# Two 512-column GpSimd reductions in place of one of 1024, and the instruction order planned anew, in a fused linear-attention and MLP kernel

## The chip, the cores and the metric

One core of one Trainium2 chip. The metric is the device time of one execution in microseconds (us). TensorE is PE in the profile, VectorE DVE, ScalarE ACT, GpSimd POOL, SyncE SP.

## What is computed

Linear attention over 8 batches, 8 heads, 576 positions and 64 columns per head, then a two-layer MLP over all 4608 tokens, all in fp32:

```python
def phi(x):
    proj = np.einsum('bhsd,df->bhsf', x, w_phi)
    proj = proj - np.max(np.abs(proj), axis=-1, keepdims=True)
    return np.concatenate([np.exp(proj), np.exp(-proj)], axis=-1)
q_p, k_p = (phi(q), phi(k))
kv = np.einsum('bhsf,bhsd->bhfd', k_p, v)
z = np.sum(k_p, axis=2)
num = np.einsum('bhsf,bhfd->bhsd', q_p, kv)
den = np.einsum('bhsf,bhf->bhs', q_p, z)[..., None] + 1e-06
x = (num / den) ...                       # (4608, 512)
h = x @ w_in                              # (4608, 2048)
out = (0.5 * h * (1.0 + erf(h / sqrt(2)))) @ w_out
```

## The kernel before

The attention goes batch by batch. `k_unit` projects keys (`pk` on PE), takes the largest magnitude (`mx`, DVE), subtracts (`ek`, DVE) and exponentiates twice (ACT); `k_quad` sums against the values (`kv` on PE). A query unit is two heads of one batch: `q_front` projects (`pq` on PE), copies to `pc` (ACT), finds the largest magnitude over the 128 partitions by one GpSimd `partition_all_reduce` into `mb` (line 511), subtracts (DVE) and exponentiates to `ef` (ACT). From batch 2 on (`b >= ND`), `q_pair` also weights `ef` by the key sums on DVE (lines 553 and 556) and `q_sum` adds over the partitions by a second `partition_all_reduce` into `db` (line 522). `pn` on PE is the numerator. Batch 0 is cut into pieces of 288 positions per head. From batch 1 on a main unit has 512 positions of each of its two heads, that is 1024 columns, and the last 64 positions of all heads make one "rest" unit of 512 columns. So 28 main units take a maximum of 1024 columns, and 24 of them a sum.

The MLP goes over 18 blocks of 256 tokens. `tokens` gathers a block and multiplies by the quotients (`xr`), and splits it into a high and a low part (`xh`, `xl`), so that three fp32r products stand for one fp32 product. `up` makes `ph` (12 products of 256 columns for 128 hidden columns), ACT takes Gelu of it into `gh` and in place, DVE takes the rest `gl`, and `po` is summed on PE. A `ph` buffer is free again when DVE has made its `gl`, and there are two. Blocks 8 to 17 (`seven`) use fewer products by a Strassen step with sums of weights (`ts`, made on DVE and ACT during blocks 2 to 7). The weights come as 64-bit floats, and `split_weight` turns each of 32 tiles into a high and a low fp32r part on DVE: two `tensor_scalar` operations (lines 391 and 393), two `scalar_tensor_tensor` (395, 397) and one subtraction. Block 0 needs them all: `w_i` for `ph`, `w_o0` to `w_o15` for `po`.

The order of instructions on every engine is made by `Plan.order`, a list scheduler in the kernel file: each operation has an engine, a cost, a rank and buffers, and the scheduler plays them through and records the order in which they would start. `emit` issues them in that order, and every engine then runs its list strictly in order. Its model has one rule on GpSimd: while one reads (`READS`, us after its start), a DVE operation with `port` set does not start.

```python
if o.eng == "dve" and o.port and port[1] <= t < port[2]:
    t = port[2]
```

Some twenty constants at the end of the file (`T0`, `AT`, `LEAD`, `BIAS`, ...) set ranks and limits.

Of the kernel before, what the change touches and what calls it, by code (L numbers as in the profile page):

```python
# [27 lines left out]
P = 128  # L28
# [4 lines left out]
TB = 256  # L33
# [29 lines left out]
class Plan:  # L63
# [21 lines left out]
    def op(self, eng, cost, fn, r=(), w=(), also=(), rank=0.0, table=None, late=0.0, kb=0, duty=1.0, kind="f", port=None, part=None, after=(), behind=()):  # L85
        o = Op()
        o.eng, o.cost, o.fn, o.rank, o.table, o.late, o.n = eng, cost, fn, rank, table, late, len(self.ops)
        o.users, o.ready, o.nbytes, o.duty, o.kind, o.part = [], self.since, kb, duty, kind, part
        o.port = port if port is not None else eng == "dve"
# [12 lines left out]
        for b in o.bufs:  # L102
            b.left += 1
        o.deps = deps
        o.wait = len(deps)
        for d in deps:
            d.users.append(o)
        if eng == "pe" and self.stream in ("k", "q"):
            o.rank += PULL
        self.ops.append(o)  # L110
        return o

    def order(self, bias):
# [56 lines left out]
        while len(done) < n:  # L170
# [38 lines left out]
                table[0] = o.table  # L209
            if o.eng == "pe":  # L210
                if self.SHAPE[last[0]] != self.SHAPE[o.kind]:
                    cost += self.BEHIND[last[0]] + self.BEFORE[o.kind]
                last[0] = o.kind
            o.start = t
            if o.eng == "pool" and o.port:
                t = max(t, port[0])
                port[1:] = [t, t + self.READS[o.port]]
# [11 lines left out]
            for b in o.bufs:  # L229
                if b.tag is not None and not b.held:  # L230
                    f = slot_free_at[b.tag]
                    b.slot = turn[b.tag]
                    f[b.slot] = None
                    turn[b.tag] = (b.slot + 1) % len(f)
                    b.held = True
                    assert b.line.pop(0) is b
                b.left -= 1
                if b.left == 0 and b.tag is not None:
                    slot_free_at[b.tag][b.slot] = o.end + o.late + self.HOP[o.eng]
            for u in o.users:  # L240
                u.wait -= 1
                u.ready = max(u.ready, o.end + o.late + (self.HOP if u.eng != o.eng else self.SAME)[o.eng] + (POOLSLACK if o.eng == "pool" else 0.0))
                if u.wait == 0:
                    cand[u.eng].append(u)
            done.append(o)
# [25 lines left out]
def dve(n, psum=False, fast=False):  # L271
    return ((62 if psum else 66) + (n / 2 if fast else n)) / 960
# [19 lines left out]
def fused_kernel(ctx: ExitStack, tc: tile.TileContext, qT, kT, va, w_st, w_in, w_out, out):  # L292
# [88 lines left out]
    def split_weight(src, nm, rank):  # L381
# [118 lines left out]
    def q_front(nm, n, load, kb, k, main):  # L500
# [18 lines left out]
    def q_sum(nm, n, pc, k, main):  # L519
        db = sb["db"]([P, 2, n], F32, f"db_{nm}")  # L520
        total = f"add{main}"
        op("pool", plan.SPENT[total], lambda: nc.gpsimd.partition_all_reduce(db(), pc()[:, :2], P, bass_isa.ReduceOp.add), r=[pc], w=[db], port=total, **k())  # L522
        return db

    def q_pair(b, p, kvs, rank, halves=(0, 1)):
# [4 lines left out]
        for half in halves:  # L530
# [20 lines left out]
            one = lambda s, j, kvn=kvn: kvn()[:, 2 * s + j, D : D + 1]  # L551
            for j in range(2):
                op("dve", dve(n, fast=True) + 0.06, lambda pc=pc, ef=ef, one=one, j=j: nc.vector.tensor_scalar(
                    out=pc()[:, j], in0=ef[0]()[:, j], scalar1=one(0, j), scalar2=None, op0=ALU.mult), r=[ef[0], kvn], w=[pc], **k())
# [58 lines left out]
    def quotients(b, half, rank):  # L613
        plan.stream = "r"
        nm = f"{b}_{half}"
        dc = sb["dc"]([P, PIECES[b][half][1] // 16], F32, f"dc_{nm}")
        spread = lambda t: t().rearrange("h (q t) -> (h q) t", q=16)
        d, r = d_d[b][half], r_d[b][half]
        op("sp", 0.06, lambda: nc.sync.dma_start(out=dc(), in_=spread(d)), r=[d], w=[dc], kb=9, rank=next(rank))
        op("dve", 0.09, lambda: nc.vector.tensor_scalar(out=dc(), in0=dc(), scalar1=SHIFT, scalar2=None, op0=ALU.add), r=[dc], w=[dc], rank=next(rank))  # L620
        op("dve", 0.19, lambda: nc.vector.reciprocal(out=dc(), in_=dc()), r=[dc], w=[dc], rank=next(rank))
# [24 lines left out]
    def tokens(j, rank):  # L646
# [7 lines left out]
        while t < (j + 1) * TB:  # L654
# [14 lines left out]
            for i in range(2):  # L669
                op("sp", 0.06, lambda b=b, i=i, h=h, s=s, n=n, o=o: nc.sync.dma_start(  # L670
                    out=xh().bitcast(F32)[64 * i : 64 * i + 64, :, o : o + n],
                    in_=r_d[b][h]()[:, s : s + n].rearrange("(c i) t -> i c t", i=2)[i : i + 1].to_broadcast([64, NCC, n])),
                   r=[r_d[b][h]], w=[xh_all], kb=n * 1.024, rank=rank(0) - 8)
            t += n
        tt("dve", dve(NCC * TB), xr, xr, lambda: xh().bitcast(F32), ALU.mult, [xr, xh_all], [xr], rank=rank(0) - 4)
        copy("dve", dve(NCC * TB, fast=True), xh, xr, [xr], [xh_all], rank=rank(0) - 4)
# [187 lines left out]
SUMSEACH = 5.49
SUMSPAN = 311.59
T15 = 926.21
T18 = 982.3
# [16 lines left out]
LEAD = 161.66
HOLD = 16.53
WR = -32.15
ATR = -58.86
AT = 194.75
# [46 lines left out]
```

## Time and profile before

| | |
|---|---|
| three runs | 1066.56, 1070.01, 1070.71 us, median 1070.01 us |
| profiled execution | 1067.51 us, span 1065.7 us |
| mean granted clock | 0.991 of full speed |
| PE busy | 1033.3 us, 97% of the span |
| DVE, ACT, POOL busy | 683.6, 615.4, 306.4 us |

The span is what the trace covers from the first to the last instruction, and all positions in it are us from its start. Busy time is the time in which at least one instruction of an engine was in flight. An instruction's recorded time includes time in which it was held up after its semaphores were there. A short fp32 product stands in the trace as two records.

### The profile page before, as it was taken

The page shows a single profiled execution, that of the slowest core. Times are in us where ns is not written, and L with a number is a line of the kernel's source. Part 1 is how long each engine was busy: PE and PEld are TensorE (multiplying, and loading weights), DVE is VectorE, ACT ScalarE, POOL GpSimd, SP SyncE. Part 2 cuts the span into 40 slices and gives each one's busy share as a digit, 9 for nine tenths or more (in the row PEclk, how much of TensorE's full clock was granted, in tenths as well). Part 3 has the DMA queues.
Part 4 walks back from the last instruction along what each step waited for, and adds up shares of the span by engine and source line. Part 5 has one row for each costly group of instructions (what it writes and reads, how often), then busy time and mean ns, then how long its engine had stood idle before and what let it go on. Part 6 is the DMA issues. An engine that isn't in the chain of part 4 may idle for free.

```text
span 1065.7 us, 23642 instructions
## 1 busy us (share of the span) xinstructions
PE 1033.3 (97%) x9765; PEld 897.1 (84%) x9765; DVE 683.6 (64%) x1228; ACT 615.4 (58%) x1006; POOL 306.4 (29%) x77
## 2 busy tenths in 40 slices
PE   6978998999999999999999999999999999999997
PEld 4645777787877888887888788999999999999997
DVE  4989998878878787435254534466465565465454
ACT  4877876767678758766665563334344344344343
POOL 2243133553655556556364661000000000000000
PEclk7999999999999999999999999999999999999999
DMA  8496562444343545223131336411111011021000
GB/s 289 125 266 181 176 200 80 131 137 140 127 139 108 150 124 156 60 84 95 42 104 27 110 111 195 171 41 41 37 44 41 25 56 38 24 60 30 11 21 21
DMA packets 87180, 107.08 MB, mean 100 GB/s; under 512 B 29168, under 2 KB 56832, under 8 KB 87072
## 3 DMA queue, kind: packets, MB, share of 16 engines
q1 hardware_dynamic: 86928, 105.30, 32.6%
q8 instruction: 77, 1.26, 0.5%
q14 instruction: 31, 0.25, 0.1%
q10 hardware_dynamic: 144, 0.26, 0.1%
HBM read 75.87 MB, written 29.66 MB: 99 GB/s over the span
## 4 chain that ended last, share of the span: by engine, by line
PE 83%; DVE 9%; DMA 3%; ACT 3%; issue 2%; SPq 1%; POOL 0%; DVEq 0%; ACTq 0%
PE ph L334 33%; PE po L334 16%; PE pa L334 10%; PE pb L334 7%; PE kv L334 6%; PE pn L334 5%; PE pk L334 3%; PE pq L334 2%; DMA xh<-r_d 1%; DVE mx L439 1%; PE pn_rest L334 1%; DVE ek L375 1%; DVE pc L375 1%; DVE w_i L375 1%; DVE ts L375 1%
## 5 line engine op out<-in xcount | busy, mean ns | idle before, releaser
L334 PE MATMUL ph<-xh,w_i 128*128 128x256 f32 x2304 | 417.6, 279 | 2.9 <-DVE gl L375 2.7
L334 PEld LDWEIGHTS ph<-xh,w_i 128*128 128x128 f32 x2304 | 357.6, 189 | 12.9 <-issue 7.6
L334 PE MATMUL ph<-xl,w_i 128*128 128x256 f32 x1152 | 319.7, 277 | 0.8 <-DVE xl L375 0.8
L334 PEld LDWEIGHTS ph<-xl,w_i 128*128 128x128 f32 x1152 | 217.1, 188 | 1.2 <-DVE xl L375 1.0
L522 POOL PARTITION_ALL_REDUCE db<-pc x24 | 151.6, 6317 | 110.6 <-DVE pc L556 105.6
L375 DVE TENSOR_TENSOR sg<-ga 128x256 f32<-128x256 f32 (+1 forms) x240 | 84.7, 376 | 144.3 <-ACT ga L780 143.5
L511 POOL PARTITION_ALL_REDUCE mb<-pc x36 | 121.4, 3373 | 187.8 <-ACT pc L369 126.2
L334 PE MATMUL po<-w_o,gh 128*128 128x512 f32 (+1 forms) x518 | 164.3, 399 | 0.2 <-ACT gh L703 0.2
L780 ACT ACTIVATE ga<-ph 128x512 f32<-128x512 f32 x80 | 47.8, 598 | 162.3 <-PE ph L334 153.6
L334 PEld LDWEIGHTS po<-w_o,gh 128*128 128x128 f32 x518 | 93.1, 188 | 32.8 <-issue 8.8
L334 PE MATMUL pa<-w_o,oh 128*128 128x256 f32 x640 | 113.0, 276 | 0.0
L334 PE MATMUL po<-w_o,gl 128*128 128x512 f32 (+1 forms) x283 | 101.0, 372 | 0.8 <-DVE gl L375 0.8
L334 PEld LDWEIGHTS pa<-w_o,oh 128*128 128x128 f32 x640 | 96.4, 188 | 0.0
L334 PE MATMUL pa<-w_o,ol 128*128 128x256 f32 x320 | 88.7, 277 | 0.4 <-DVE ol L375 0.4
L334 PE MATMUL pn<-ef,kvn 128*64 128x512 f32 (+2 forms) x288 | 81.1, 563 | 7.0 <-ACT xo L369 4.8
L334 PE MATMUL pb<-tw,uh 128*128 128x256 f32 x480 | 85.8, 276 | 1.2 <-ACT oh L369 1.2
L375 DVE TENSOR_TENSOR gl<-ph,gh 128x512 fp32r<-128x512 f32 x64 | 43.9, 687 | 64.8 <-ACT ph L704 61.8
L516 ACT ACTIVATE ef<-pc 128x1024 f32<-128x1024 f32 (+1 forms) x72 | 68.3, 972 | 15.2 <-DVE pc L375 14.8
L444 ACT ACTIVATE ek<-ek 128x1024 f32<-128x1024 f32 x64 | 67.6, 1058 | 14.6 <-DVE ek L375 14.0
L334 PEld LDWEIGHTS pb<-tw,uh 128*128 128x128 f32 x480 | 72.3, 188 | 1.4 <-issue 1.4
L369 ACT CAST uh<-sg 128x384 fp32r<-128x384 f32 x80 | 41.3, 516 | 46.5 <-DVE sg L375 46.5
L334 PE MATMUL kv<-vt,ek 128*64 128x65 f32 x2048 | 66.5, 224 | 0.7 <-ACT ek L444 0.7
(84 smaller groups left out, 1584.1 us busy)
## 6 DMA issues: line engine op xcount, KB each, us to landing
vt<-in_va_dram SPq DMA_DIRECT2D x32, 325.0 KB
t_d<-ts SPq DMA_DIRECT2D x40, 256.0 KB
out_dram<-ob SPq DMA_DIRECT2D x35, 256.0 KB
kt<-in_kT_dram SPq DMA_DIRECT2D x32, 256.0 KB
raw_i<-in_w_in_dram SPq DMA_DIRECT2D x16, 512.0 KB
raw_o<-in_w_out_dram SPq DMA_DIRECT2D x16, 512.0 KB
qt<-in_qT_dram SPq DMA_DIRECT2D x28, 256.0 KB
x_d<-xo SPq DMA_DIRECT2D x24, 256.0 KB
```

Of the source, the lines that this page charges most:

```text
L334: return tc.keep_in_program_order(nc.tensor.matmul(*a, **kw))
L369: op(eng, cost, lambda: nc.scalar.copy(out=dst(), in_=src()), r=r, w=w, **kw)
L375: op(eng, cost, lambda: e.tensor_tensor(out=dst(), in0=a(), in1=b(), op=o), r=r, w=w, **kw)
L439: op("dve", dve(256 * n, True), lambda: nc.vector.tensor_reduce(out=mx(), in_=xs(), axis=AX.X, op=ALU.max, apply_absolute_value=True), r=[ ...
L444: op("act", act(256 * n), lambda s=s: nc.scalar.activation(e[s](), e[1](), AF.Exp, scale=1.0 - 2.0 * s), r=[e[1]], w=[e[s]], table="exp", ...
L511: op("pool", plan.SPENT[most], lambda: nc.gpsimd.partition_all_reduce(mb(), pc(), P, bass_isa.ReduceOp.absmax), r=[pc], w=[mb], port=most, ...
L516: op("act", act(2 * n), lambda s=s: nc.scalar.activation(ef[s](), pc(), AF.Exp, scale=1.0 - 2.0 * s), r=[pc], w=[ef[s]], table="exp", **k())
L522: op("pool", plan.SPENT[total], lambda: nc.gpsimd.partition_all_reduce(db(), pc()[:, :2], P, bass_isa.ReduceOp.add), r=[pc], w=[db], port= ...
L780: op("act", act(2 * TB, True) + 0.037, lambda ph=ph, ga=ga: nc.scalar.activation(ga(), ph(), AF.Gelu), r=[ph_all], w=[ga], table="gelu", a ...
```

## The change

1. In `q_front` and `q_sum`, the maximum and the sum of a main unit are two `partition_all_reduce` of 512 columns each (one per head) in place of one of 1024. Units of 288 positions and rest units stay as they are. No other instruction's work changes.
2. The scheduler's model: a GpSimd reduction now also has a window in which it writes (`WRITES`), in which DVE operations marked `port=2` (the fast one-input ones) do not start, and the window in which it reads gets new numbers. The reciprocal no longer counts as an operation that can be held. Switching shapes on PE has another price, small slacks are added to what PE waits for, the broadcast load of the quotients counts three times the bytes, and the constants at the end are new.

```diff
-    READS = {"max": 1.2, "add": 2.45, "max main": 2.15, "add main": 4.45, "max rest": 1.1, "add rest": 2.2}
+    READS = {"max": 1.15, "add": 2.45, "max main": 2.1, "add main": 4.43, "max rest": 1.05, "add rest": 2.15}
+    WRITES = {"max": (1.4, 2.02), "add": (2.75, 3.47), "max main": (2.3, 3.42), "add main": (4.6, 5.97), "max rest": (1.2, 1.83), "add rest": (2.4, 3.1)}
...
-            if o.eng == "dve" and o.port and port[1] <= t < port[2]:
-                t = port[2]
+            if o.eng == "dve":
+                for a, z, least in port[1:]:
+                    if o.port >= least and a <= t < z:
+                        t = z
...
-        op("pool", plan.SPENT[most], lambda: nc.gpsimd.partition_all_reduce(
-            mb(), pc(), P, bass_isa.ReduceOp.absmax), r=[pc], w=[mb], port=most, **k(1))
+        if main == " main":
+            for j in range(2):
+                op("pool", plan.SPENT["max rest"], lambda j=j: nc.gpsimd.partition_all_reduce(
+                    mb()[:, j], pc()[:, j], P, bass_isa.ReduceOp.absmax), r=[pc], w=[mb], port="max rest", **k(1))
+        else:
...
+        if main == " main":
+            for j in range(2):
+                op("pool", plan.SPENT["add rest"], lambda j=j: nc.gpsimd.partition_all_reduce(
+                    db()[:, j], pc()[:, j], P, bass_isa.ReduceOp.add), r=[pc], w=[db], port="add rest", **k())
+        else:
...
-BIAS = 103.27
+BIAS = 170.63
...
-T0 = 91.27
+T0 = 86.42
```

On POOL, the main units of batch 2 (a name is `mb` or `db`, batch, pair of heads, piece and a running number; batches count from 0; `x2` stands for two equal rows). Before:

```order
L511 ISA mb_2_0_0_1732<-pc_2_0_0_1720 128x1024
L511 ISA mb_2_1_0_1834<-pc_2_1_0_1752 128x1024
L522 ISA db_2_0_0_1941<-pc_2_0_0_1720 128x1024
L522 ISA db_2_1_0_2202<-pc_2_1_0_1752 128x1024
L511 ISA mb_2_2_0_2268<-pc_2_2_0_2261 128x1024
L511 ISA mb_2_3_0_2317<-pc_2_3_0_2280 128x1024
L522 ISA db_2_2_0_2408<-pc_2_2_0_2261 128x1024
L522 ISA db_2_3_0_2564<-pc_2_3_0_2280 128x1024
```

Now:

```order
L521 ISA mb_2_0_0_1790<-pc_2_0_0_1770 128x512 x2
L521 ISA mb_2_1_0_1870<-pc_2_1_0_1815 128x512 x2
L537 ISA db_2_0_0_2013<-pc_2_0_0_1770 128x512 x2
L537 ISA db_2_1_0_2210<-pc_2_1_0_1815 128x512
L521 ISA mb_2_2_0_2248<-pc_2_2_0_2240 128x512
L537 ISA db_2_1_0_2210<-pc_2_1_0_1815 128x512
L521 ISA mb_2_2_0_2248<-pc_2_2_0_2240 128x512
L521 ISA mb_2_3_0_2383<-pc_2_3_0_2365 128x512 x2
L537 ISA db_2_2_0_2497<-pc_2_2_0_2240 128x512 x2
```

Here the sum of unit 1 and the maximum of unit 2 alternate by halves, so that the maximum is complete only after half a sum that stands between its own halves. There are four such places in the new order (unit 1 and 2 of batches 2, 3, 4 and 7), and in three more a rest unit's maximum stands between the halves of a sum.

On DVE, just ahead of `gl_6` of block 0 (the operation that frees the `ph` buffer for the first products of block 1). Before:

```order
L556 SCALAR_TENSOR_TENSOR pc_0_0_1720<-ef_0_0_1_1855,kvn_0_0_1582,pc_0_0_1720 128x512
L375 TENSOR_TENSOR w_i_3_1937<-wt_i_3_1838,w_i_3_1937 128x512
L439 TENSOR_REDUCE mx_1_1_1948<-pk_1_1_1872 128x8
L375 TENSOR_TENSOR ek_1_1_1_1965<-pk_1_1_1872,mx_1_1_1948 128x1024
L393 TENSOR_SCALAR wt_o_1885<-wt_o_1885 128x512
L391 TENSOR_SCALAR wt_o_1950<-wt_o_1950 128x512
L395 SCALAR_TENSOR_TENSOR wt_o_1885<-raw_o_1717,wt_o_1885 128x512
L393 TENSOR_SCALAR wt_o_1950<-wt_o_1950 128x512
L375 TENSOR_TENSOR gl_6_2022<-ph_6_1952,gh_6_1994 128x512
```

Now:

```order
L575 SCALAR_TENSOR_TENSOR pc_0_0_1770<-ef_0_0_1_1891,kvn_0_0_1242,pc_0_0_1770 128x512
L383 TENSOR_TENSOR w_i_3_1961<-wt_i_3_1889,w_i_3_1961 128x512
L399 TENSOR_SCALAR wt_o_2005<-wt_o_2005 128x512
L575 SCALAR_TENSOR_TENSOR pc_0_0_1770<-ef_0_0_1_1891,kvn_0_0_1242,pc_0_0_1770 128x512
L401 TENSOR_SCALAR wt_o_2005<-wt_o_2005 128x512
L447 TENSOR_REDUCE mx_r<-pk_r 128x4
L383 TENSOR_TENSOR er_1_2035<-pk_r,mx_r 128x512
L403 SCALAR_TENSOR_TENSOR wt_o_2005<-raw_o_1665,wt_o_2005 128x512
L383 TENSOR_TENSOR pc_1_0_1815<-pc_1_0_1815,mb_1_0_1870 128x1024
L383 TENSOR_TENSOR gl_6_2083<-ph_6_2017,gh_6_2067 128x512
```

Before, both fast operations of line 393 and 391, then one of 395 and one of 393, stand between `ek` and `gl_6`, right after the operation of line 556 that lets the first sum of 1024 columns start. Now one fast operation (line 401, the old 393) stands there, and then two that read PSUM (`mx_r`, `er`), the old 395 and the subtraction `pc_1_0`. The numbers of the lines are 8 to 19 higher in the new file.

On DVE, at the first of the four places, the subtraction that waits for both halves of `mb_2_0`, and what stands around it. Now:

```order
L383 TENSOR_TENSOR ts_0_2272<-ts_0_2272 128x256
L383 TENSOR_TENSOR ts_1_2357<-w_o_1575 128x512
L383 TENSOR_TENSOR ts_1_2357<-ts_1_2357 128x256
L383 TENSOR_TENSOR pc_2_0_2240<-pc_2_0_2240,mb_2_0_2248 128x1024
L383 TENSOR_TENSOR gl_1_2367<-ph_1_2143,gh_1_2352 128x512
L383 TENSOR_TENSOR ts_0_2272<-ts_0_2272 128x256
L383 TENSOR_TENSOR ts_1_2357<-ts_1_2357 128x256
```

Before, the same subtraction stood between operations on `ts`, with no `gl` behind it:

```order
L375 TENSOR_TENSOR ts_1_2286<-w_o_1506 128x512
L375 TENSOR_TENSOR ts_0_2265<-ts_0_2265 128x256
L375 TENSOR_TENSOR ts_1_2286<-ts_1_2286 128x256
L375 TENSOR_TENSOR pc_2_0_2261<-pc_2_0_2261,mb_2_0_2268 128x1024
L375 TENSOR_TENSOR ts_1_2286<-ts_1_2286 128x256
L439 TENSOR_REDUCE mx_0_0_2319<-pk_0_0_2289 128x8
L375 TENSOR_TENSOR ek_0_0_1_2336<-pk_0_0_2289,mx_0_0_2319 128x1024
```

`gl_1` of block 1, which PE waits for, has come to stand right behind that subtraction.

## Rows read from the trace of the kernel before

**Rows 1.** The page's first part: busy time of each engine, its share of the span, instructions.
```profile
PE 1033.3 (97%) x9765; PEld 897.1 (84%) x9765; DVE 683.6 (64%) x1228; ACT 615.4 (58%) x1006; POOL 306.4 (29%) x77
```

**Rows 2.** Busy time of each engine in four stretches (us from the span's start : us, length, then busy time and instructions of PE, its weight loads, DVE, ACT, POOL, then granted TensorE clock, DMA share, GB/s).
```profile
0.00:20.00 20.00, 12.49 (x60) 7.26 (x60) 7.10 (x10) 8.18 (x13) 4.47 (x6) 0.80 0.85 300
20.00:182.00 162.00, 146.33 (x1654) 105.09 (x1655) 152.12 (x230) 127.35 (x199) 45.94 (x14) 0.97 0.61 179
182.00:690.00 508.00, 504.90 (x4797) 415.54 (x4796) 317.59 (x454) 329.97 (x468) 255.98 (x57) 1.00 0.38 115
690.00:1066.00 376.00, 369.57 (x3258) 369.18 (x3257) 206.80 (x537) 149.88 (x328) 0.00 (x0) 1.00 0.12 36
```

**Rows 3.** The longest waits of DVE (in total) from 20 to 182 us (engine, line, what it waited for: us in total, times, longest).
```profile
DVE w_i L375 <- ACT w_i L369: 3.0, 2, 2.2
```

**Rows 4.** DVE and POOL in order of time, taken from several stretches: start, us, engine, line, operation, out<-in, [idle before <-who ended it].
```profile
74.69 0.69 DVE L375 TENSOR_TENSOR w_i<-wt_i,w_i 128x512 fp32r<-128x512 f32 x1 [2.25 <-ACT w_i L369]
...
76.73 0.42 DVE L391 TENSOR_SCALAR wt_i<-wt_i 128x512 f32<-128x512 f32 x1
...
162.28 2.30 DVE L393 TENSOR_SCALAR wt_o<-wt_o 128x512 uint32<-128x512 uint32 x1
164.50 1.65 DVE L391 TENSOR_SCALAR wt_o<-wt_o 128x512 f32<-128x512 f32 x1
...
71.86 3.99 POOL L511 PARTITION_ALL_REDUCE mb<-pc  x1 [5.14 <-ACT pc L369]
...
103.86 3.54 POOL L511 PARTITION_ALL_REDUCE mb<-pc  x1 [8.29 <-ACT pc L369]
...
159.39 6.48 POOL L522 PARTITION_ALL_REDUCE db<-pc  x1 [4.96 <-DVE pc L556]
...
221.73 2.02 POOL L511 PARTITION_ALL_REDUCE mb_rest<-pc_rest  x1
231.11 3.27 POOL L522 PARTITION_ALL_REDUCE db_rest<-un_rest  x1 [7.36 <-DVE un_rest L375]
```

**Rows 5.** Groups of DVE instructions from 0 to 182 us, different shapes apart (line, engine, operation, out<-in, shapes, count | busy us, mean ns of one | idle before).
```profile
L391 DVE TENSOR_SCALAR wt_o<-wt_o 128x512 f32<-128x512 f32 x16 | 9.4, 585 | 0.0
...
L391 DVE TENSOR_SCALAR wt_i<-wt_i 128x512 f32<-128x512 f32 x16 | 7.9, 504 | 0.0
...
L393 DVE TENSOR_SCALAR wt_o<-wt_o 128x512 uint32<-128x512 uint32 x16 | 8.6, 537 | 0.2
L393 DVE TENSOR_SCALAR wt_i<-wt_i 128x512 uint32<-128x512 uint32 x16 | 8.5, 539 | 0.1
...
L397 DVE SCALAR_TENSOR_TENSOR wt_o<-raw_o,wt_o 128x512 uint32<-128x512 uint32 x16 | 13.8, 864 | 0.2
...
L397 DVE SCALAR_TENSOR_TENSOR wt_i<-raw_i,wt_i 128x512 uint32<-128x512 uint32 x16 | 10.8, 684 | 0.1
```

**Rows 6.** The chain of work that ended last, at 167 us, and what one unit of 24 `ph` products and one of `kv` takes on it later (start, us, what).
```profile
167.01 0.69 DVE gl L375
...
350.78 2.72 PE ph L334 x24
...
354.56 2.48 PE kv L334 x80
```

**Rows 7.** PE in order of time at that place.
```profile
167.74 0.39 PE L334 MATMUL ph<-xh,w_i 128*128 128x256 f32 x1 [2.66 <-DVE gl L375]
```

**Rows 8.** Granted clock (the share after the five engines) in two stretches after it, columns as in Rows 2.
```profile
168.00:172.00 4.00, 4.00 (x25) 4.00 (x25) 4.00 (x7) 3.08 (x5) 0.00 (x0) 0.65 0.40 119
172.00:176.00 4.00, 4.00 (x49) 3.48 (x49) 3.97 (x9) 2.42 (x5) 0.00 (x0) 0.92 0.00 0
```

**Rows 9.** More groups of DVE instructions from 0 to 182 us: those that the new order adds or moves ahead of late weights.
```profile
L375 DVE TENSOR_TENSOR er<-pk_r,mx_r 128x512 f32<-128x512 f32 x3 | 2.1, 686 | 0.0
...
L439 DVE TENSOR_REDUCE mx<-pk 128x8 f32<-128x1024 f32 x12 | 14.6, 1216 | 2.7 <-PE pk L334 2.7
...
L375 DVE TENSOR_TENSOR ek<-pk,mx 128x1024 f32<-128x1024 f32 x12 | 14.6, 1219 | 0.4
...
L375 DVE TENSOR_TENSOR gl<-ph,gh 128x512 fp32r<-128x512 f32 x8 | 5.5, 682 | 1.7 <-ACT ph L704 1.7
...
L556 DVE SCALAR_TENSOR_TENSOR pc<-ef,kvn,pc 128x512 f32<-128x512 f32 x4 | 3.0, 742 | 0.0
```

**Rows 10.** PE in order of time around the first products of block 0 (the time from one row's start to the next row's start is what the unit takes).
```profile
88.26 1.13 PE L334 MATMUL pq<-qt,wst 64*128 64x512 f32 x4
89.32 0.38 PE L334 MATMUL ph<-xh,w_i 128*128 128x256 f32 x1
...
110.50 0.70 PE L334 MATMUL pq_rest<-qt_rest,wst 64*128 64x256 f32 x4
111.14 0.38 PE L334 MATMUL ph<-xh,w_i 128*128 128x256 f32 x1
...
114.43 1.16 PE L334 MATMUL pk<-wst,kt 64*128 64x128 f32 x16
```

**Rows 11.** ACT table loads before the `Gelu` line from 0 to 182 us.
```profile
L703 ACT ACT_TABLE_LOAD x5 | 6.4, 1283 | 0.1
```

**Rows 12.** The two longest waits of PE from 182 us to the end.
```profile
PE pb L334 <- ACT oh L369: 1.2, 1, 1.2
PE po L334 <- DVE gl L375: 0.8, 1, 0.8
```

More of the change, by code (lines that the diff above doesn't have):

```diff
@@ L78, in __init__, with turn @@
     def __init__(self, tc):
+        self.banks = ("ph", "po", "pp", "kv", "pn")
         self.tc, self.ops, self.slots, self.lines, self.stream, self.since = tc, [], {}, {}, None, 0.0
+    def turn(self, a, b):
+        return self.BEHIND[a] + self.BEFORE[b] + (0.09 if a == "f" and b != "d" else 0.0)
     def pool(self, pool, tag, bufs):
@@ L88, in op @@
         o.users, o.ready, o.nbytes, o.duty, o.kind, o.part = [], self.since, kb, duty, kind, part
-        o.port = port if port is not None else eng == "dve"
+        o.port = port if port is not None else int(eng == "dve")
         o.reopen = bool(after)
@@ L211, in order @@
                 if self.SHAPE[last[0]] != self.SHAPE[o.kind]:
-                    cost += self.BEHIND[last[0]] + self.BEFORE[o.kind]
+                    cost += self.turn(last[0], o.kind)
                 last[0] = o.kind
@@ L216, in order @@
                 t = max(t, port[0])
-                port[1:] = [t, t + self.READS[o.port]]
+                a, z = self.WRITES[o.port]
+                port[1:] = [(t, t + self.READS[o.port], 1), (t + a, t + z, 2)]
             o.end = run(t, cost, o.duty) if o.eng == "pe" else t + cost
@@ L238, in order @@
                 if b.left == 0 and b.tag is not None:
-                    slot_free_at[b.tag][b.slot] = o.end + o.late + self.HOP[o.eng]
+                    slot_free_at[b.tag][b.slot] = o.end + o.late + self.HOP[o.eng] + (PESLACK if b.tag in self.banks else 0.0)
             for u in o.users:
                 u.wait -= 1
-                u.ready = max(u.ready, o.end + o.late + (self.HOP if u.eng != o.eng else self.SAME)[o.eng] + (POOLSLACK if o.eng == "pool" else 0.0))
+                u.ready = max(u.ready, o.end + o.late + (self.HOP if u.eng != o.eng else self.SAME)[o.eng] + (POOLSLACK if o.eng == "pool" else 0.0) + (PESLACK if u.eng == "pe" and o.eng != "pe" else 0.0))
                 if u.wait == 0:
@@ L354, in fused_kernel @@
     idle = sb["gl"]([P, 512], F32, "idle")
-    op("dve", dve(512, fast=True), lambda: nc.vector.memset(idle(), 0.0), w=[idle], rank=-500.0)
+    op("dve", dve(512, fast=True), lambda: nc.vector.memset(idle(), 0.0), w=[idle], rank=-500.0, port=2)
     op("act", act(1), lambda: nc.scalar.activation(idle()[:, :1], idle()[:, :1], AF.Exp), r=[idle], w=[idle], table="exp", rank=-500.0)
@@ L510, in q_front @@
         most = f"max{main}"
-        op("pool", plan.SPENT[most], lambda: nc.gpsimd.partition_all_reduce(
-            mb(), pc(), P, bass_isa.ReduceOp.absmax), r=[pc], w=[mb], port=most, **k(1))
+        if main == " main":
[3 more added lines that the diff above has]
+        else:
+            op("pool", plan.SPENT[most], lambda: nc.gpsimd.partition_all_reduce(
+                mb(), pc(), P, bass_isa.ReduceOp.absmax), r=[pc], w=[mb], port=most, **k(1))
         tt("dve", dve(2 * n), pc, pc, mb, ALU.subtract, [pc, mb], [pc], **k(1))
@@ L521, in q_sum @@
         total = f"add{main}"
-        op("pool", plan.SPENT[total], lambda: nc.gpsimd.partition_all_reduce(db(), pc()[:, :2], P, bass_isa.ReduceOp.add), r=[pc], w=[db], port=total, **k())
+        if main == " main":
[3 more added lines that the diff above has]
+        else:
+            op("pool", plan.SPENT[total], lambda: nc.gpsimd.partition_all_reduce(
+                db(), pc()[:, :2], P, bass_isa.ReduceOp.add), r=[pc], w=[db], port=total, **k())
         return db
@@ L553, in q_pair @@
                 op("dve", dve(n, fast=True) + 0.06, lambda pc=pc, ef=ef, one=one, j=j: nc.vector.tensor_scalar(
-                    out=pc()[:, j], in0=ef[0]()[:, j], scalar1=one(0, j), scalar2=None, op0=ALU.mult), r=[ef[0], kvn], w=[pc], **k())
+                    out=pc()[:, j], in0=ef[0]()[:, j], scalar1=one(0, j), scalar2=None, op0=ALU.mult), r=[ef[0], kvn], w=[pc], port=2, **k())
             for j in range(2):
@@ L619, in quotients @@
         op("sp", 0.06, lambda: nc.sync.dma_start(out=dc(), in_=spread(d)), r=[d], w=[dc], kb=9, rank=next(rank))
-        op("dve", 0.09, lambda: nc.vector.tensor_scalar(out=dc(), in0=dc(), scalar1=SHIFT, scalar2=None, op0=ALU.add), r=[dc], w=[dc], rank=next(rank))
-        op("dve", 0.19, lambda: nc.vector.reciprocal(out=dc(), in_=dc()), r=[dc], w=[dc], rank=next(rank))
+        op("dve", 0.09, lambda: nc.vector.tensor_scalar(out=dc(), in0=dc(), scalar1=SHIFT, scalar2=None, op0=ALU.add), r=[dc], w=[dc], port=2, rank=next(rank))
+        op("dve", 0.19, lambda: nc.vector.reciprocal(out=dc(), in_=dc()), r=[dc], w=[dc], port=0, rank=next(rank))
         op("sp", 0.06, lambda: nc.sync.dma_start(out=spread(r), in_=dc()), r=[dc], w=[r], kb=9, rank=next(rank))
@@ L672, in tokens @@
                     in_=r_d[b][h]()[:, s : s + n].rearrange("(c i) t -> i c t", i=2)[i : i + 1].to_broadcast([64, NCC, n])),
-                   r=[r_d[b][h]], w=[xh_all], kb=n * 1.024, rank=rank(0) - 8)
+                   r=[r_d[b][h]], w=[xh_all], kb=n * 3.0, rank=rank(0) - 8)
             t += n
         tt("dve", dve(NCC * TB), xr, xr, lambda: xh().bitcast(F32), ALU.mult, [xr, xh_all], [xr], rank=rank(0) - 4)
-        copy("dve", dve(NCC * TB, fast=True), xh, xr, [xr], [xh_all], rank=rank(0) - 4)
+        copy("dve", dve(NCC * TB, fast=True), xh, xr, [xr], [xh_all], rank=rank(0) - 4, port=2)
         tt("dve", dve(NCC * TB), xl, xr, lambda: xh().bitcast(F32), ALU.subtract, [xr, xh_all], [xl_all], rank=rank(0) - 4)
@@ L863 @@
 SUMSAT = 177.8
[L864 to L867, printed above, removed]
-BIAS = 103.27
+SUMSEACH = 5.25
+SUMSPAN = 452.38
+T15 = 954.63
+T18 = 988.07
+BIAS = 170.63
 STICK = 2
-PATIENCE = 2.16
+PATIENCE = 2.13
 URGE = -1000.0
-EARLY = 40.11
-WPACE = 4.91
-WSPAN = 36.41
+EARLY = 43.22
+WPACE = 4.75
+WSPAN = 36.91
 WARM = 4
@@ L878 @@
 ND = 2
-LUMP = 5.52
-LINGER = 3.07
+LUMP = 4.8
+LINGER = 4.54
 PAIR_K = 0.224
@@ L883 @@
 PULL = -2000.0
[L884 to L888, printed above, removed]
+LEAD = 175.51
+HOLD = 22.02
+WR = -39.77
+ATR = -104.6
+AT = 170.89
+PESLACK = 0.03
 POOLSLACK = 0.3
-DMASLACK = 0.3
-T0 = 91.27
+DMASLACK = 0.08
+T0 = 86.42
 RATE = 285.0
```

6 lines of the change are left out of this document (3 added, 3 removed).

## The prediction

> **What bounds the kernel now.** The page's first part [rows 1] has PE busy for 97% of the span. Busy time is no proof that an engine is the limit, so the next view is the table of stretches [rows 2]; the reader is to subtract PE's busy time from each stretch. PE is idle for 7.5 us of the first 20, for 162.00 - 146.33 = 15.7 us from 20 to 182, for 3.1 us from 182 to 690, and for 6.4 us after that, where most is the tail behind the last product. So once the ramp is over, at about 182 us, PE is the limit, and no change on POOL, DVE or ACT is worth more than some 3 us there. In the ramp another engine limits: DVE is busy 152.12 of 162.00 us, ACT 127.35, POOL 45.94. DVE's longest wait there is one for ACT of 3.0 us in total [rows 3], so DVE's list of work sets the pace: 32 weight tiles, and the attention of the first batches between them. What can be gained lies in DVE's time in the ramp, and what can be lost lies there or in a new wait of PE later.
>
> DVE's busy time in the ramp isn't all work. A fast one-input operation of 512 columns took 0.42 us at 76.73 us, and one took 2.30 us and the next 1.65 us at 162.28 us, while POOL ran a sum of 6.48 us from 159.39 us [rows 4]. In the groups of the stretch [rows 5], the four groups of fast operations have means of 504 to 585 ns; against 420 ns that is 16 x (0.165 + 0.084 + 0.117 + 0.119) = 7.8 us held. Line 397 on `wt_o` has 864 ns against 684 ns for the same shape on `wt_i`: 16 x 0.18 = 2.9 us. Together 10.7 us are held time, all next to POOL's reductions.
>
> One such place reaches PE. On the chain of waits [rows 6], `gl` of 0.69 us at 167.01 us stands behind those two held operations, and PE waits 2.66 us for it [rows 7]. Then the granted clock falls from 1.00 to 0.65 for four us and 0.92 for four more [rows 8], that is to the lower of its two levels (1.2 GHz, not 2.4) for part of the time: 4 x 0.35 + 4 x 0.08 = 1.7 us of full-speed work lost. The place costs 4.4 us in all.
>
> **The change, part by part.**
>
> *Two reductions for one.* A maximum of 1024 columns took 3.54 us and one of 512 columns 2.02 us; a sum took 6.48 and 3.27 us [rows 4]. So a main unit's maximum goes to 4.04 us (+0.5) and its sum to 6.54 us (+0.06). The cover: DVE hardly waits for POOL in the ramp (no such wait is among its longest [rows 3]), because the order leaves other work between a maximum and its subtraction. I take 0. If that cover were gone, the six main maxima up to 182 us would cost 6 x 0.5 = 3.0 us.
>
> *The held operations ahead of `gl_6`.* The first held operation was let go at 162.28 + 2.30 - 0.42 = 164.16 us, 4.8 us after the sum had started, and the two lost 1.88 + 1.23 = 3.1 us [rows 4]. Now one fast operation stands there, then two that read PSUM, then a `scalar_tensor_tensor` and the subtraction `pc_1_0`. By the same proportion a sum of 512 columns lets go after about 2.4 us (an estimate, 4.8 x 3.27 / 6.48). What can be held ahead of `gl_6` is then between 0 and 2.4 us; I take the middle, 1.2, since it isn't known where in the second half the subtraction arrives. PE's wait falls by 3.1 - 1.2 = 1.9 us to some 0.75 us. A wait of 0.8 us for `gl` later [rows 12] left the clock of its stretch at 1.00 [rows 2], so the 1.7 us of the clock go too: -3.6 us. The bounds are 0 and -4.4 us. What is late next is the weights of `w_o12` to `w_o15`, which stand on the same DVE list behind the same place, so not all of it is kept: I take -2.6 us.
>
> *The other held time,* 10.7 - 3.1 = 7.6 us. The new windows keep the fast operations away from a reduction's end, and no reduction locks for longer than a half; but there are twice as many, and the list is fixed while the times drift. I take 0, with a bound of -4 us.
>
> *Work moved ahead of the last weights.* Ahead of `w_o14` DVE now also does `er`, `mx`, `ek`, one `gl` and two operations of `pc`: 0.69 + 1.22 + 1.22 + 0.68 + 2 x 0.74 = 5.3 us [rows 9]. Ahead of the products that use it, PE now also does a `pk` unit (1.16 us), a `pq` unit (1.06 us) and 24 `ph` products (2.72 us), 4.9 us [rows 6, 10]. The net is +0.4 us. Ahead of `w_o12` DVE has +1.9 us (`er`, `mx`, a reduction of `er`'s size, less one operation of line 395, taken as 0.68 like line 397) and PE +3.6 us (a `pk` and a `kv` unit): -1.7 us. So the longer DVE list is matched by PE work moved along with it, and I take 0. SP's list follows (keys and values of batch 2 are fetched ahead of some weights); the DMA engines were busy 0.61 of that stretch [rows 2] and no wait for them is among DVE's longest, which is the cover.
>
> *Changes of kind on PE.* The order has 227 of them for 233. A `pq` unit of 512 columns takes 1.06 us from start to start and one of 256 columns 0.64 us [rows 10], so 256 columns cost 0.42 us and 0.22 us is left for changing over. Six fewer are worth up to 1.3 us; since dear and cheap pairs of kinds are exchanged too, I take -0.6.
>
> *ACT.* The new order has 13 table loads ahead of the last weight's cast where there were 9, at 1.28 us each [rows 11], 5.1 us. ACT has 162.00 - 127.35 = 34.7 us idle in the ramp [rows 2], which covers them: 0. Without it, +5.1.
>
> The sum is -2.6 - 0.6 = -3.2 us on the profiled execution of 1067.5 us: 1064.3 us. That execution stands 2.5 us under the median of the runs shown, 1070.0, so the forecast in their terms is **1066.8 us**. About 0.5%, 5.3 us, is what a measurement can tell from no change, so this counts as no change, on the faster side.
>
> **The rivals.**
>
> *Most of the held time goes.* For it: 7.8 of the 10.7 us are fast operations, which the new windows are about; and the ramp's 15.7 us of PE idle leave room. Against it: the times drift from the plan, as the holds before show. Then -4.4 - 3.5 - 0.6 = -8.5 us: 1061.5 us.
>
> *The split buys nothing.* A hold that lasted as long as the reduction would make two halves worse than one, by 6 x 0.5 us and a little in the ramp. Of POOL's 45.94 us there, DVE felt 10.7, or 23%, so 3.1 us more would cost 0.7 us, and the place at `gl_6` stays: -0.6 + 0.7 = +0.1 us, 1070.1 us. Against it: `w_i` at 74.69 us, with two inputs in SBUF, ran in 0.69 us within a maximum of 3.99 us that had begun at 71.86 us, and the operation at 162.28 us was let go 1.7 us before its sum ended [rows 4]. The Trainium skill, "SBUF — State Buffer", section "SBUF: two separate sides", states this rule: the pair of ports that VectorE and GpSimd share is an exclusive lock that the first comer holds for the whole instruction. By that rule the sum would be this rival's; the two rows speak against "whole".
>
> *A maximum that waits for half a sum (slower).* At four places a main maximum now has half a sum between its halves, so it comes 3.27 us later [rows 4]. DVE runs its list in order: at the first such place `gl_1` of block 1 stands right behind the subtraction that waits, and PE needs `gl_1`. It decides where PE has less work queued than DVE stands. With 1 us queued, such a place costs 2.3 us and, if the clock falls as in [rows 8], 1.7 more: 4.0 us. Two places give +8 us, three +12; the middle is 1066.8 + 10 = 1077 us. For it: the two rows stand next to each other in the list. Against it: the order puts other DVE work ahead of the subtraction, and from 182 to 690 us DVE is idle for 190 of 508 us [rows 2].
>
> **How the numbers follow.** The forecast gets 0.45 with a range of its own of 1063 to 1070 us (holds ahead of `gl_6` from 0 to 2.4 us, moved work from -1.7 to +0.4). Most of the held time going gets 0.21, the split buying nothing 0.15, the late maximum 0.19. The whole range is 1059 to 1076 us; it leaves out the far ends of the first and the last rival. Faster by over 0.5% (under 1064.7 us) takes the first rival and a quarter of the forecast, 0.32; slower by over 0.5% (over 1075.4 us) takes most of the last rival and a little of the second, 0.17; 0.51 is left between.
>
> **What would show it.** Right: PE's idle time from 20 to 182 us is 12 to 14 us instead of 15.7; the fast operations' means in the groups fall towards 450 ns; no wait of PE for `gl` over 1 us near 167 us, and no dip of the clock after it; from 182 to 690 us PE stays idle for about 3 us. Wrong: a PE wait for `gl` of block 1 or later of over 1 us with a subtraction on DVE waiting for `mb` ahead of it; DVE waits for `mb` of some us in total; or line 391 and 393 held as before, then the split did nothing.

## The result and the profile after

The changed kernel takes 1078.43 us (median of 4 runs, 1077.83 to 1079.43), the kernel before 1070.36 us beside it: ratio 1.0074, 95% interval 1.0046 to 1.0101. It is **slower**, by 0.7%; the forecast was 1066.8 us with a range of 1059 to 1076. The profiled execution took 1078.5 us with a span of 1076.7.

The first view is the page's first part, against [rows 1]:

```profile
PE 1033.8 (96%) x9771; PEld 895.8 (83%) x9771; DVE 705.1 (65%) x1228; ACT 623.6 (58%) x1012; POOL 334.5 (31%) x129
```

PE does the same work. POOL is 28 us busier with its 52 added instructions, and DVE, whose count is unchanged, is 21.5 us busier. Next the stretches, columns as in [rows 2], with that from 182 to 690 us cut at 430, and below them the two pieces of the kernel before:

```profile
20.00:182.00 162.00, 144.79 (x1670) 104.92 (x1670) 150.99 (x228) 129.40 (x200) 50.80 (x22) 0.97 0.61 181
182.00:430.00 248.00, 236.31 (x2356) 187.05 (x2354) 207.14 (x274) 178.27 (x254) 143.05 (x53) 0.99 0.40 125
430.00:690.00 260.00, 260.00 (x2336) 216.55 (x2333) 123.52 (x165) 152.53 (x207) 136.20 (x50) 1.00 0.34 104
```

```profile
182.00:430.00 248.00, 246.83 (x2614) 199.23 (x2613) 201.21 (x279) 177.10 (x258) 136.35 (x31) 1.00 0.44 132
430.00:690.00 260.00, 258.07 (x2185) 216.31 (x2184) 116.38 (x175) 152.87 (x211) 119.63 (x27) 1.00 0.33 100
```

The loss is in the middle row: from 182 to 430 us PE is idle for 248.00 - 236.31 = 11.7 us where it was idle for 1.2. From 430 to 690 us it isn't idle at all. From 20 to 182 us it is idle for 17.2 us, 1.5 more than before. The two longest waits of PE after 182 us (engine, line, what it waited for: us in total, times, longest), against [rows 12]:

```profile
PE po L342 <- DVE gl L383: 5.0, 4, 2.4
PE ph L342 <- DVE gl L383: 2.0, 1, 2.0
```

So DVE is late with `gl`. Which of its groups grew? One, the multiply-add that writes a unit's `pc` for the sum. Before and now:

```profile
L556 DVE SCALAR_TENSOR_TENSOR pc<-ef,kvn,pc 128x512 f32<-128x512 f32 x48 | 36.5, 783 | 0.0
```

```profile
L575 DVE SCALAR_TENSOR_TENSOR pc<-ef,kvn,pc 128x512 f32<-128x512 f32 x48 | 57.0, 1203 | 0.0
```

Those 20.5 us are nearly all that DVE gained. A mean of 1203 ns hides short operations and long ones, which the order of time shows. Here are DVE at three places of batches 3 and 4, and POOL at the first:

```profile
251.50 0.73 DVE L575 SCALAR_TENSOR_TENSOR pc<-ef,kvn,pc 128x512 f32<-128x512 f32 x1
...
252.50 2.72 DVE L575 SCALAR_TENSOR_TENSOR pc<-ef,kvn,pc 128x512 f32<-128x512 f32 x1
...
255.75 0.68 DVE L383 TENSOR_TENSOR gl<-ph,gh 128x512 fp32r<-128x512 f32 x1
...
293.15 2.72 DVE L575 SCALAR_TENSOR_TENSOR pc<-ef,kvn,pc 128x512 f32<-128x512 f32 x1
...
335.57 2.73 DVE L575 SCALAR_TENSOR_TENSOR pc<-ef,kvn,pc 128x512 f32<-128x512 f32 x1
...
252.33 6.59 POOL L537 PARTITION_ALL_REDUCE db<-pc  x2 [3.49 <-DVE pc L575]
```

Here the first multiply-add of a unit (head 0) takes 0.73 us, the second (head 1) 2.72 us. The sum's first half starts at 252.33 us, right after the first one wrote head 0, and 0.17 us before the second one starts. Before, the sum of 1024 columns needed both heads and could only start behind both. The scheduler in the kernel knows buffers, not halves of them: it plans both halves of the sum behind both multiply-adds. On the chip this half started when its own half of `pc` was there, and the multiply-add that writes the other half was held. In batches 2 to 4 eight of the twelve units show such a hold, of 1.1 to 2.0 us. The sums of the other four waited for an earlier `db` to be sent off by DMA, and so began no sooner than about the end of the second multiply-add, which took 0.74 us or less there.

What this costs PE is seen at the first such place, the one of [rows 6] and [rows 7]. The chain of waits that ended last (start, us, what):

```profile
163.45 2.65 DVE pc L575
166.10 0.72 DVE wt_o L401
166.83 0.60 DVE mx_r L447
...
167.52 0.70 DVE er L383
...
168.25 0.65 ACT er L452
...
169.55 1.28 ACT L722
...
170.85 0.60 ACT gh L722
171.44 0.50 ACT ph L723
...
171.97 0.70 DVE gl L383
...
172.71 6.01 PE ph L342 x36
```

The held multiply-add delays `er`, ACT's exponentials wait for it, behind these stand a table load and the two passes of `ph`, and `gl` comes at 171.97. PE waited 2.53 us for it,

```profile
172.71 0.39 PE L342 MATMUL ph<-xh,w_i 128*128 128x256 f32 x1 [2.53 <-DVE gl L383]
```

and its granted clock (after the five engines; columns as in [rows 8]) was part of the time at the lower of its two levels:

```profile
172.00:176.00 4.00, 3.29 (x20) 3.29 (x21) 4.00 (x7) 3.97 (x6) 0.00 (x0) 0.73 0.51 135
176.00:180.00 4.00, 4.00 (x26) 3.78 (x26) 4.00 (x9) 2.77 (x5) 0.00 (x0) 0.84 0.00 0
```

### The profile page after: what moved, and what is told of

The parts are those of the page before. It is cut to its first block, busy times and chain, and to the rows that moved or that the text cites. A ratio compares the mean times of both kernels' runs of the same rounds, so it can differ in the third digit from the quotient of the medians.

```text
span 1076.7 us, 23713 instructions
## 1 busy us (share of the span) xinstructions
PE 1033.8 (96%) x9771; PEld 895.8 (83%) x9771; DVE 705.1 (65%) x1228; ACT 623.6 (58%) x1012; POOL 334.5 (31%) x129
## 4 chain that ended last, share of the span: by engine, by line
PE 76%; DVE 12%; ACT 5%; DMA 3%; issue 3%; POOL 0%; SPq 0%; DVEq 0%; ACTq 0%
PE ph L342 33%; PE po L342 12%; PE pa L342 10%; PE pb L342 7%; PE kv L342 4%; PE pn L342 4%; PE pk L342 2%; DVE ts L383 2%; PE pq L342 2%; DVE mx L447 1%; DVE pc L383 1%; DMA dc<-d_d 1%; DVE ek L383 1%; ACT ek L452 1%; DVE pc L575 1%
## 5 line engine op out<-in xcount | busy, mean ns | idle before, releaser
L537 POOL PARTITION_ALL_REDUCE db<-pc x48 | 165.4, 3480 | 97.5 <-DVE pc L575 72.9
L521 POOL PARTITION_ALL_REDUCE mb<-pc x56 | 115.8, 2110 | 109.3 <-ACT pc L377 60.7
L342 PEld LDWEIGHTS po<-w_o,gl 128*128 128x128 f32 x288 | 54.1, 188 | 20.1 <-DVE gl L383 8.6
```

Source lines behind the costliest of these rows:

```text
L342: return tc.keep_in_program_order(nc.tensor.matmul(*a, **kw))
L521: op("pool", plan.SPENT["max rest"], lambda j=j: nc.gpsimd.partition_all_reduce(mb()[:, j], pc()[:, j], P, bass_isa.ReduceOp.absmax), r=[p ...
L537: op("pool", plan.SPENT["add rest"], lambda j=j: nc.gpsimd.partition_all_reduce(db()[:, j], pc()[:, j], P, bass_isa.ReduceOp.add), r=[pc], ...
```

## The experiments

Theory A: the early start of the first half of a sum makes the loss. Rival B: maxima that stand between halves of sums (the prediction's slower rival). Rival C: the new order as such. Rival D: two operations cost more than one. Each kernel was timed against the kernel before on the same chip; ratios have 95% intervals.

**1. Four kernels that take the parts apart.** The changed kernel with one edit, which leaves the order on every engine as it is:

```diff
-            for j in range(2):
+            for j in (1, 0):
                 op("pool", plan.SPENT["add rest"], ...
```

> The changed kernel with the two halves of a main unit's sum issued in the other order (head 1 first). The plan, and the order on every other engine, stay as they are; the first half of the sum now needs the half of pc that DVE writes last, so it can't start while DVE still writes. Theory A (the first half of the sum starts as soon as the first half of pc is written, and holds DVE's second multiply-add of pc for some 2 us; DVE's backlog makes gl late): that group's mean falls from 1203 ns to 780 to 850 ns, TensorE's idle time from 182 to 690 us falls from 11.7 to 3 to 6 us, and the kernel takes 1064 to 1071 us. Rival B (maxima that stand between halves of sums), rival C (the new order and constants as such) and rival D (two operations cost more than one): 1076 to 1081 us, since none of them changes.

Measured: 1067.64 us, ratio 0.9991 (0.9975 to 1.0006). The early start is worth 0.83% of the time, 8.9 us (by the two intervals, some 0.3% either way), and with it gone the changed kernel is no slower than before. The group, and the same place in order of time:

```profile
L575 DVE SCALAR_TENSOR_TENSOR pc<-ef,kvn,pc 128x512 f32<-128x512 f32 x48 | 38.4, 816 | 0.0
```

```profile
163.65 0.74 DVE L575 SCALAR_TENSOR_TENSOR pc<-ef,kvn,pc 128x512 f32<-128x512 f32 x1
164.31 0.41 DVE L401 TENSOR_SCALAR wt_o<-wt_o 128x512 uint32<-128x512 uint32 x1
164.65 0.68 DVE L447 TENSOR_REDUCE mx_r<-pk_r 128x4 f32<-128x512 f32 x1
...
166.04 1.34 DVE L403 SCALAR_TENSOR_TENSOR wt_o<-raw_o,wt_o 128x512 uint32<-128x512 uint32 x1
...
169.87 0.69 DVE L383 TENSOR_TENSOR gl<-ph,gh 128x512 fp32r<-128x512 f32 x1 [1.36 <-ACT ph L723]
```

The same instructions, started within 0.3 us of the same time; the multiply-add takes 0.74 us where it took 2.73, and `gl` comes 2.1 us sooner. PE waits 0.18 us for it, and from 172 to 180 us the granted clock is 1.00.

```profile
170.62 0.38 PE L342 MATMUL ph<-xh,w_i 128*128 128x256 f32 x1 [0.18 <-DVE gl L383]
```

By stretches (columns as in [rows 2]):

```profile
20.00:182.00 162.00, 147.90 (x1680) 106.96 (x1680) 148.94 (x228) 131.01 (x203) 50.30 (x22) 0.96 0.60 181
182.00:430.00 248.00, 243.51 (x2449) 194.24 (x2451) 204.66 (x278) 184.59 (x260) 152.12 (x56) 1.00 0.41 127
```

PE is idle for 14.1 and 4.5 us, against 17.2 and 11.7 in the changed kernel and 15.7 and 1.2 before. So not all of the loss from 182 to 430 us is the early start's. PE's waits that are left from 160 us on:

```profile
PE ph L342 <- DVE gl L383: 2.2, 2, 2.0
PE pq L342 <- issue: 1.6, 1, 1.6
PE po L342 <- DVE gl L383: 1.5, 2, 1.1
```

The wait of 2.0 us of `ph`, in the changed kernel's list above too, is as long as it was: it comes with the new order.

The split alone, in the kernel before, with the scheduler left to plan the halves by its old rules and constants:

> The kernel before with the split of maxima and sums alone: model and constants as before (a half is costed as a rest unit's reduction). Theory A: the sums read early here as well, so the second multiply-add of pc is held again (group mean above 1100 ns) and the kernel is slower than before by 3 to 12 us, 1073 to 1082 us. Rival B: only 3 places where a main unit's maximum is interleaved with a sum; 1070 to 1074 us. Rival C (the loss is in the new order): 1068 to 1072 us, no change. Rival D: as the changed kernel, 1075 to 1081 us, but with the group near 783 ns.

> As the split alone in the kernel before, with the two halves of the sum issued in the other order, so that neither can start before both halves of pc are written. Theory A: the multiply-add's mean back at 780 to 850 ns, and 1066 to 1072 us. Rival B and rival D: as the split alone, within 1.5 us of it. Rival C: 1068 to 1072 us, as the split alone.

Measured: 1084.53 us (1.0142, 1.0117 to 1.0166), and with the halves the other way round 1076.15 us (1.0068, 1.0047 to 1.0089). The first is above every range, A's by 2.5 us. The difference of the two, in one order, is 0.74%: theory A again, the group's mean going from 1196 to 782 ns. But 0.7% stay, which A doesn't explain (it missed the second too, by 4 us) and D (no change from the first to the second) doesn't either. What is left to differ is the order that the old rules make of halves: in the second kernel PE is idle for 19.2 us from 20 to 182 us and for 5.9 from there to 430. What in that order does it was not taken apart.

The changed model and constants without the split:

> The changed kernel's model and constants, without the split: one reduction of 1024 columns for a main unit's maximum and one for its sum, which need both halves of pc. Theory A: the multiply-add's mean at 780 to 850 ns, 1063 to 1071 us. Rival C (the new model and constants make the loss): 1075 to 1082 us. Rivals B and D: 1066 to 1071 us, as theory A.

Measured: 1075.99 us (1.0059, 1.0036 to 1.0082). A, B and D missed here, C was right: new rules and constants with whole reductions also make an order that costs 0.6%. So an order planned with the split alone loses, and one planned with the new rules alone does too; that is a loss of its own, apart from the early start.

**2. The same orders, other reductions.** To keep the order fixed, whole reductions were put into the changed kernel's order, at the second half's place, and halves into the old one, where `halves` issues the two behind each other (lines shortened):

```diff
 # new order, whole (also for db)
-    lambda j=j: nc.gpsimd.partition_all_reduce(mb()[:, j], pc()[:, j], P, ...)
+    lambda j=j: [] if j == 0 else nc.gpsimd.partition_all_reduce(mb(), pc(), P, ...)
 # old order, halves (also for mb); the other kernel has (1, 0)
-    lambda: nc.gpsimd.partition_all_reduce(db(), pc()[:, :2], P, ...)
+    lambda: halves(bass_isa.ReduceOp.add, db, pc, (0, 1))
```

> The order of the kernel before, instruction by instruction on all engines, with each reduction of a main unit issued as two halves back to back, head 0 first. Theory A: the second multiply-add is held as in the changed kernel (group mean 1150 to 1250 ns) and the kernel is 6 to 12 us slower than before, 1075 to 1082 us. Rival C (the loss comes from the new order alone): 1068 to 1071 us.

> As the split in the order of before, with the sum's halves issued head 1 first, so that neither starts before both halves of pc are written. Theory A: mean 780 to 850 ns, and 1066 to 1071 us, within 2 us of before. Rival D (two operations for one cost something of their own): 2 us or more above before.

Measured: 1078.73 us (1.0090, 1.0064 to 1.0116) and 1067.07 us (0.9989, 0.9974 to 1.0005), on one chip. In the old order too the early start costs 1.0%, and the split without it neither costs nor gains anything that the interval could tell. So rival D doesn't hold. The group in the one and in the other:

```profile
L570 DVE SCALAR_TENSOR_TENSOR pc<-ef,kvn,pc 128x512 f32<-128x512 f32 x48 | 56.1, 1189 | 0.0
```

```profile
L570 DVE SCALAR_TENSOR_TENSOR pc<-ef,kvn,pc 128x512 f32<-128x512 f32 x48 | 35.5, 760 | 0.0
```

> The changed kernel's order, instruction by instruction on all engines, with one reduction of 1024 columns in place of the two halves, at the second half's place; nothing else differs. A whole sum needs both halves of pc. Theory A (the early start of the first half sum is the whole loss; the split itself and the new order are worth nothing): as with the sum held back until both halves are written, 1065 to 1070 us, multiply-add's mean 780 to 850 ns. Rival C (this order fits halves only: a whole sum holds DVE for more of its time at once and ends later): 1072 to 1078 us, as the new plan with whole reductions.

> The changed kernel's order with halved maxima as they are and whole sums at the second half's place. It tells what made the same order with both whole so slow (1087.2 us). If the whole sums did (the order puts DVE's fast operations where the plan has a gap between two halves, and the whole sum's longer hold catches them): 1080 to 1088 us. If the whole maxima did (they end later and DVE stands in the subtraction): 1066 to 1072 us.

Measured: 1087.22 us (1.0172, 1.0148 to 1.0197), and with whole sums alone 1084.79 us (1.0153, 1.0125 to 1.0181). A missed the first by 17 us and C by 9: this order can't do with whole sums, and the second run says that it is mainly they, not the whole maxima. One place of the second of them, DVE and POOL:

```profile
230.12 5.03 DVE L383 TENSOR_TENSOR pc_rest<-pc_rest,mb_rest 128x512 f32<-128x512 f32 x1 [0.53 <-POOL mb_rest L524]
...
228.15 1.94 POOL L524 PARTITION_ALL_REDUCE mb_rest<-pc_rest  x1 [13.60 <-ACT pc_rest L377]
229.99 6.19 POOL L537 PARTITION_ALL_REDUCE db<-pc  x1
```

The order puts DVE's subtraction right behind a maximum that a sum follows, and a whole sum holds it for 5.03 - 0.68 = 4.4 us. That is one place. From 160 to 430 us at least ten operations of DVE take 2.4 us or more in this trace, and PE is idle for 14.6 us from 182 to 430; what each of them costs was not taken apart.

**3. Where a held microsecond counts.** Head 1 first in batches 2 to 4 alone:

> The changed kernel with the sum's halves issued head 1 first in batches 2 to 4 alone, whose sums run up to some 400 us; in batches 5 to 7 the sum still starts early and holds DVE (7.5 us of held time over the middle of the group there in the changed kernel, against 14.7 us in batches 2 to 4). Theory A with the place (only a hold while TensorE waits for gl, before 430 us, costs anything): all of the gain, 1066 to 1069 us. If every held us costs alike: two thirds of the gain, 1070 to 1073 us.

Measured: 1068.96 us (1.0010, 0.9991 to 1.0030). The median is in the range for all of the gain, but the interval also holds two thirds of it (1.0074 - 0.0055 = 1.0019), so the time doesn't decide. The stretches speak for the place. From 430 to 690 us, with the early start in batches 5 to 7 and, below, without it (the first experiment's kernel):

```profile
430.00:690.00 260.00, 260.00 (x2358) 219.74 (x2357) 127.15 (x178) 150.04 (x210) 126.53 (x47) 1.00 0.35 105
```

```profile
430.00:690.00 260.00, 260.00 (x2343) 219.87 (x2339) 122.73 (x178) 149.35 (x210) 123.55 (x47) 1.00 0.34 105
```

DVE is busy for 4.4 us longer with it, and PE is idle in neither.

**4. Constants searched anew.** If the plan is right where no sum starts earlier than planned, it can be searched by its own total, the time at which the scheduler's model ends. A random search over the constants lowered it, for three versions:

```diff
 # halved maxima, whole sums (the first of the three)
-PATIENCE = 2.13
+PATIENCE = 0.937
-AT = 170.89
+AT = 182.556
-T0 = 86.42
+T0 = 95.31
...
```

> The changed kernel with whole sums (which need both halves of pc) and halved maxima, and with 13 of the plan's constants searched anew so that the plan's own total falls: 1055.0 us, against 1062.9 for the changed kernel's plan and 1072.4 for the new plan with whole reductions. Those two measured 4 to 5 us above their plan's total where nothing started earlier than planned (1067.6 and 1076.0 us). Theory A (the plan is right once no sum starts early): 1057 to 1063 us, faster than before. Rival (the search only fits what the plan has wrong): 1064 to 1074 us.

> Maxima and sums halved with the sum's halves issued head 1 first, and 9 constants of the plan searched anew: the plan's own total is 1057.5 us against 1062.9 before the search. Theory A: 1060 to 1065 us. Rival (the search only fits what the plan has wrong): 1066 to 1074 us.

> Whole reductions under the changed model, 7 constants searched anew: the plan's own total is 1059.2 us against 1072.4. Theory A: 1061 to 1067 us, so 2 us or more above the halved maxima with whole sums if halving the maxima is worth something. Rival: 1068 to 1076 us.

Measured: 1061.55 us (0.9947, 0.9926 to 0.9968), 1067.01 us (0.9997, 0.9979 to 1.0015) and 1064.82 us (0.9977, 0.9962 to 0.9992). The first beats both kernels; A was right for it and for the third and missed the second, where the plan's gain of 5.4 us didn't arrive. The first by stretches:

```profile
182.00:430.00 248.00, 247.48 (x2465) 201.33 (x2465) 193.27 (x280) 176.52 (x255) 133.38 (x40) 1.00 0.41 125
```

PE is idle for 0.5 us, with DVE 13.9 us less busy than in the changed kernel. What of this the halved maxima do isn't shown. The third has the reductions of the fourth kernel of part 1, and the constants alone brought it from 1.0059 to 0.9977. The searches changed 13, 9 and 7 constants, so the 3.3 us between the first and the third don't price the halved maxima either.

## Why the prediction was wrong

**The step that failed** is "two reductions for one", taken as 0. It priced how long two halves run (two halves of a sum take 6.59 us in the place shown), and did not ask when the first may start; the cover that it named was that of the maximum alone. The old sum waited for both multiply-adds; a half waits for one. The listing of DVE's order showed the second multiply-add behind other work, so there was room for the half to start in. Price found: 0.83% in the new order (8.9 us), 1.0% in the old, where 0 was taken.

**The bound.** Nothing in the runs speaks against DVE setting the pace in the ramp (150.99 of 162.00 us busy). That it has slack after the ramp did not hold where it mattered: "idle for 190 of 508 us" is a mean over two stretches. From 182 to 430 us DVE was busy for 201.21 of 248.00 us already before, and after it for 116.38 of 260.00. In the first stretch DVE's lateness reached PE, in the second none of it did.

**The held operations ahead of `gl_6`,** -2.6 us. The two fast operations went from there as foretold, but the multiply-add of `pc`, which the text counted as work, is held for 2.0 us in their place: the wait of 2.53 us and the dip of the clock stayed. With the early start taken away, what is held ahead of `gl_6` is 1.34 - 0.68 = 0.66 us (1.2 was taken), the clock stays at 1.00, and PE's idle time up to 182 us is 14.1 us, in the 12 to 14 that the text named, nearly. So the term's mechanism was right and its condition, that no other operation ahead of `gl_6` is held, was not.

**The other held time,** 0. The means of lines 399 and 401, the fast operations, are now 487, 457, 452 and 556 ns for 585, 504, 537 and 539 [rows 5]: 16 x 0.213 = 3.4 us less. Lines 403 and 405 rose:

```profile
L405 DVE SCALAR_TENSOR_TENSOR wt_i<-raw_i,wt_i 128x512 uint32<-128x512 uint32 x16 | 13.8, 860 | 0.2
L403 DVE SCALAR_TENSOR_TENSOR wt_i<-raw_i,wt_i 128x512 uint32<-128x512 uint32 x16 | 11.9, 742 | 0.4
L403 DVE SCALAR_TENSOR_TENSOR wt_o<-raw_o,wt_o 128x512 uint32<-128x512 uint32 x15 | 11.7, 782 | 0.1
L405 DVE SCALAR_TENSOR_TENSOR wt_o<-raw_o,wt_o 128x512 uint32<-128x512 uint32 x15 | 11.2, 746 | 0.1
```

Their counterparts before are line 397 [rows 5] and line 395 (680 ns on `wt_o`, 683 on `wt_i`). The four means add up to 3130 ns for 2911, 16 x 0.219 = 3.5 us more. The term of 0 came out by luck, as two changes that cancel. With the early start taken away the four fast means add up to 2032 ns for 2165 and the four others to 2948 for 2911, so that 16 x 0.096 = 1.5 us of held time go: most of the rise was the early start's as well, and the rival "most of the held time goes", which took 3.5 us here, was too hopeful.

**Moved work, changes of kind, ACT.** No run tests these alone. With the early start taken away the kernel stands at 0.9991 (0.9975 to 1.0006) of before, where the sum of all terms was -3.2 us, 0.9970: together they brought less than forecast, by some 2 us. The stretches tell where: PE's idle time fell by 1.6 us in the ramp, and by 1.9 from 430 to 690 us, but it rose from 1.2 to 4.5 us from 182 to 430 us, where the sum of terms had nothing. Of the 4.5, 2.0 us are one wait of the new order (next paragraph); which terms the rest belongs to stays open.

**The rivals.** The slower one, 1077 us, gave nearly the right time by the wrong road. The changed kernel and the one with head 1 first have the same waits of DVE for a maximum,

```profile
DVE pc L383 <- POOL mb L521: 7.9, 4, 4.3
```

yet one is 8.9 us faster than the other, and none of these waits lies between 182 and 430 us, where PE lost its time. The fastest kernel has 14.1 us of them. At the place that the prediction named, PE does wait 2.0 us for `gl_1`, in both kernels, but not because of the maximum. In the changed kernel, POOL and the chain of waits:

```profile
194.75 2.02 POOL L521 PARTITION_ALL_REDUCE mb<-pc  x1
```

```profile
199.53 1.22 DVE pc L383
200.74 0.61 DVE gl L383
```

The maximum was complete at about 196.77 us, 2.8 us before DVE came to the subtraction. It is the subtraction's own 1.22 us, and the work ahead of it, that stand before `gl_1`. That the split buys nothing is so in the old order with head 1 first (0.9989). The reason given for that rival is not borne out: the Trainium skill, "SBUF — State Buffer", section "SBUF: two separate sides", has the lock last for the whole instruction, and this case's trace does not agree: there a held operation was let go about 4.5 us into a sum of 6.19 us (last section).

## What to carry to other kernels

Cutting an operation in two changes not only how long it runs but what it waits for: list, for each half, the write it now depends on and what its engine's neighbour does right after that write. Where the first half may start too soon, issue first the half that is written last; that one line was worth 0.7 to 1.0% here. And read how busy an engine is in the stretch where its consumer waits, since a mean over two stretches hides the one that has less slack.

## What the runs showed of the hardware

A GpSimd sum over partitions held DVE operations for only part of its time, in both places read here: one of 512 columns that began at 252.33 us let the multiply-add go at about 252.50 + 2.72 - 0.73 = 254.49 us, 2.2 us later, in the pair's 6.59 us; a whole one that began at 229.99 us let the subtraction go at about 230.12 + 5.03 - 0.68 = 234.47 us, 4.5 us later, of 6.19. Both times take it that the operation ran for its usual time once it was let go. The held operation is not only a fast one-input one: a multiply-add of two SBUF inputs that started 0.17 us after the sum was held for 2.0 us, and a subtraction of two inputs for 4.4. The prediction counted a two-input operation (line 397) among the held ones, but took the multiply-add for work.
